# Keys and queries of the kept tokens: transposed by DMAs in place of VectorE

## The chip, the cores and the metric

The kernel runs on one core of a Trainium2 chip. That core has TensorE (matmuls; the profile calls it PE, its weight loads PEld), VectorE (DVE), ScalarE (ACT), GpSimd (POOL) and SyncE (SP), which issues DMAs. The five work side by side and wait for each other only by semaphores. The metric is the device time of one execution in microseconds; the time before is the median of 3 runs, 836.36 us (834.82 to 839.12).

## The reference

Two attention blocks read the same 2048 tokens of width 512, and a gate mixes them. Block A walks over 64 segments of 32 tokens, one after the other, because each hands 8 memory rows to the next:

```python
for s in range(n_seg):                       # 64
    xs = x[:, s*seg_len:(s+1)*seg_len, :]
    h = jnp.concatenate([mem, xs], axis=1)   # 8 memory rows + 32 tokens
    q = jnp.einsum('btd,dhe->bhte', h, Wq)   # 32 heads of 128; k and v alike
    scores = jnp.einsum('bhqe,bhke->bhqk', q, k) * scale
    scores = jnp.where(mask[None, None], scores, -1e9)
    o = jnp.einsum('bhqk,bhke->bhqe', _softmax(scores, axis=-1), v)
    o = jnp.einsum('bhte,hed->btd', o, Wo)
    mem = o[:, :M, :]
    outs.append(o[:, M:, :])
```

Block B is a causal attention with 32 heads of 16 within each of four stretches of 512 tokens, plus a running sum over the stretches before. The output is `g * a + (1 - g) * b`, with `g` a sigmoid of `x` times `gate_w`. All inputs are bf16.

## The kernel before

**Two kinds of tokens.** Of a segment's 40 rows (8 of memory, 32 tokens) the kernel takes 32 through the serial path: the 24 first tokens and the 8 memory rows, `hT`. The last 8 tokens of each segment do not depend on the memory until the scores, so their projections are made ahead, for four segments at a time: group `j` (0 to 15) holds the 4 x 8 last tokens of segments 4j to 4j+3. GpSimd gathers them into `xr` (`p_xr`), and `p_rest(j, kind, r)` projects them, for `kind` k, q or v and for `r`, the half of the heads (16 heads, 2048 columns).

**A projection.** `wproj` (L1389) makes it: the 32 tokens are the stationary side in four column tiles, so that partition 32g + t of the result holds token t and the g-th of four column sets of 512. For v a set is 512 neighbouring columns, four whole heads. For k and q a set is 32 of each head's 128 columns, for all 16 heads.

**The staging ring.** The result is copied out of PSUM (L995, by ScalarE or VectorE) into one of three staging buffers `stg`, taken in turn by `stage()`. The ring also serves block B's transposed keys (`bkn`, L1077), the second half of the output projection of the kept tokens (`parr`) and the rows of the final mix (`ain`, `fin`). For v a DMA stores the buffer to DRAM (`rvst`, L1361); it comes back spread over the segments as `rem_v` (`rlv`, L1398). For k and q VectorE transposes it in blocks of 32 x 32 (L1375) straight into `rem_k` or `rem_q`, 8 slots of [128, 256], one slot a segment, so that group j fills one half of the slots and group j+1 the other.

**A segment.** `p_seg(s)` copies the segment's kept queries out of `rem_q` into columns 32 to 39 of `QT` with one GpSimd copy (`qr`, L1422); the kept keys are read by TensorE where they lie in `rem_k` (L1464). Keys and queries of `hT` are projected, copied to `st` and transposed by VectorE (L1445). The scores `S` are the matmuls of L1460 and L1464. Then follow the exponentials (L1468), the sums `U` (L1483), their reciprocals on ScalarE (L1487, L1489), the multiplications (L1491 on VectorE, L1494 `nrr` on either VectorE or GpSimd), `PV` (L1525, L1530), the output projection (L1294), and `fold` and `hm` (L1018, L1317), which put the 8 new memory rows into the next `hT`.

**What sets the order.** Every operation is described once with its reads and writes. A planner can put them in order from costs written beside each (`cost`, and `load` for a DMA); here the order is given: `ORDER` is a packed table with one list for each engine, and each engine takes its list strictly in turn. An operation that either of two engines may do belongs to the one in whose list it stands. A slot of PSUM in pool "F" makes its first matmul wait for all that the later operations of the slot wait for, so a projection into a staging buffer that is not yet free holds TensorE's list. Operations on one named resource (`rem_k` of a parity, `stg1`, `qTr`) wait for each other.

```python
sl = P.slot("F" if j else "A")
P.op("dve", lambda d: d.transpose(dst, st[:, :].rearrange("p (h s k) -> p h s k", s=4, k=8)), reads=[rs],
     writes=["rem%s%d" % (kind, j % 2)], name="r%stp%d_%d" % (kind, j, r), cost=T_TP, prio=prio)
```

## Time and profile before

The profile shows one execution, which took 832.18 us, 830.2 us of them between its first and last instruction.

| what | us |
|---|---|
| median of 3 runs (lowest to highest) | 836.36 (834.82 to 839.12) |
| the profiled execution: time, span | 832.18, 830.2 |
| PE busy, share of the span | 805.0, 97% |
| PEld busy, share | 520.7, 63% |
| DVE busy, share | 623.3, 75% |
| ACT busy, share | 557.7, 67% |
| POOL busy, share | 256.8, 31% |
| the 64 transposes of kept keys and queries, VectorE (L1375) | 22.1 + 22.3 |
| the 64 copies of kept queries, GpSimd (L1422) | 27.4 |

A busy share is the union of an engine's instructions. Ends of matmuls are modelled and matmuls overlap, so a busy PE is not one at its peak. A row of waits reads "who waited <- for whom: us in total, times, longest us". A row of an instruction gives shortest, median and longest duration in ns, the first and last start in us, and its shape. "issue" is waiting that the profile can't put down to anyone. SyncE's entries are marked SPq: they issue DMAs and are not busy time.

### The profile page before, as it was taken

The numbers are of one execution on the slowest core, as the hardware profiler recorded it, in microseconds if no ns is written. First come the engines' busy times: TensorE is split into PE (matmuls) and PEld (weight loads), VectorE is DVE, ScalarE is ACT, GpSimd is POOL, SyncE is SP. The second block draws the span as 40 slices with busy tenths as digits, with TensorE's granted clock in tenths as the row PEclk, the third lists the DMA queues.
The fourth block names the chain that finished last, engine by engine and source line by source line (L and its number), as shares of the span: only waits on it lengthen the run. The fifth ranks groups of instructions, "written<-read, shape, count | busy, mean of one in ns | idle before, by whom it ended". The sixth has DMA issues, their size and how long they took to land.

```text
span 830.2 us, 53252 instructions
## 1 busy us (share of the span) xinstructions
PE 805.0 (97%) x24462; PEld 520.7 (63%) x24462; DVE 623.3 (75%) x1417; ACT 557.7 (67%) x1264; POOL 256.8 (31%) x572
## 2 busy tenths in 40 slices
PE   8999999999999999999999999999999999998988
PEld 4446666666566666666666666666666666665655
DVE  4878667778778778677787787777777867777776
ACT  3667666777667766667666767677677666666663
POOL 3453221333232323322322422423313314333240
PEclk9999999999999999999999999999999999999999
DMA  9983101111111110211012111101111100001001
GB/s 345 412 249 61 45 17 39 39 45 23 47 27 28 39 26 19 50 34 44 25 39 43 39 27 32 41 18 32 32 36 33 40 25 12 21 19 26 10 22 36
DMA packets 71700, 45.62 MB, mean 55 GB/s; under 512 B 50046, under 2 KB 69942, under 8 KB 69942
## 3 DMA queue, kind: packets, MB, share of 16 engines
q1 hardware_dynamic: 70422, 41.18, 17.2%
q8 instruction: 192, 3.15, 1.6%
q10 hardware_dynamic: 1056, 1.05, 0.4%
q14 instruction: 30, 0.25, 0.1%
HBM read 30.72 MB, written 8.87 MB: 48 GB/s over the span
## 4 chain that ended last, share of the span: by engine, by line
PE 82%; DMA 6%; DVE 4%; ACT 4%; SPq 2%; issue 1%; POOL 0%; DVEq 0%; POOLq 0%
PE pb L1389 45%; PE pb L1294 16%; PE pb L1018 7%; DMA Wo_sb<-in_A_Wo_dram 4%; PE pb L1135 3%; PE pb L1525 3%; PE pb L1020 2%; PE pb L1176 2%; PE pb L1483 2%; PE pb L1460 1%; SPq L891 1%; DMA rest_v<-stg 1%; DMA wqB_sb<-in_B_wq_dram 1%; PE pb L1224 1%; ACT rc_sb L1489 1%
## 5 line engine op out<-in xcount | busy, mean ns | idle before, releaser
L995 ACT ACTIVATE st<-pb 128x512 bf16<-128x512 f32 (+2 forms) x309 | 147.0, 495 | 115.8 <-PE pb L1389 96.4
L1153 ACT ACTIVATE PTB<-pb 128x640 bf16<-128x640 f32 x240 | 159.3, 703 | 46.3 <-PE pb L1135 37.3
L1389 PE MATMUL pb<-Wv_sb,hT 128*32 128x512 bf16 x2048 | 160.0, 379 | 0.0
L1389 PE MATMUL pb<-Wq_sb,hT 128*32 128x256 bf16 (+1 forms) x3072 | 139.0, 308 | 0.4 <-DVE hT L1317 0.4
L1389 PE MATMUL pb<-Wk_sb,hT 128*32 128x512 bf16 x2048 | 134.1, 379 | 0.7 <-DVE phiK L1204 0.7
L1294 PE MATMUL pb<-Wo_sb,OT_sb 128*32 128x256 bf16 x4096 | 130.7, 273 | 1.3 <-issue 0.8
L1294 PEld LDWEIGHTS pb<-Wo_sb,OT_sb 128*32 128x32 bf16 x4096 | 101.3, 96 | 14.3 <-ACT OT_sb L995 2.2
L1389 PEld LDWEIGHTS pb<-Wq_sb,hT 128*32 128x32 bf16 x3072 | 83.6, 97 | 41.1 <-issue 1.1
L1159 POOL TENSOR_SCALAR_AFFINE_SELECT PTB<-PTB 128x512 bf16<-128x512 bf16 x120 | 77.0, 642 | 95.6 <-ACT PTB L1153 89.2
L1445 DVE STREAM_TRANSPOSE QT_sb<-st 128x256 bf16<-128x256 bf16 (+1 forms) x192 | 94.1, 508 | 9.2 <-ACT st L995 7.4
L1445 DVE STREAM_TRANSPOSE KT_sb<-st 128x512 bf16<-128x512 bf16 x128 | 89.3, 700 | 12.4 <-ACT st L995 10.3
L1494 POOL TENSOR_TENSOR PT_sb<-PT_sb,rc_sb 128x64 bf16<-128x64 bf16 x87 | 32.0, 368 | 212.1 <-ACT rc_sb L1489 203.6
L1389 PEld LDWEIGHTS pb<-Wk_sb,hT 128*32 128x32 bf16 x2048 | 57.1, 97 | 44.0 <-issue 2.1
L995 ACT ACTIVATE OT_sb<-pb 128x320 bf16<-128x320 f32 (+1 forms) x141 | 57.8, 426 | 35.9 <-PE pb L1530 34.5
L995 DVE CAST OT_sb<-pb 128x320 bf16<-128x320 f32 (+1 forms) x119 | 56.5, 481 | 22.6 <-PE pb L1530 21.7
L1389 PEld LDWEIGHTS pb<-Wv_sb,hT 128*32 128x32 bf16 x2048 | 51.8, 96 | 18.5 <-ACT st L995 0.2
L1317 DVE CAST hT<-pb 128x32 bf16<-128x32 f32 x63 | 12.0, 190 | 68.3 <-PE pb L1018 68.1
L1487 ACT ACTIVATE rc_sb<-pb 128x160 f32<-128x160 f32 x128 | 38.9, 304 | 32.7 <-PE pb L1483 31.8
L1468 ACT ACTIVATE PT_sb<-pb 128x224 bf16<-128x224 f32 x128 | 45.4, 356 | 14.7 <-PE pb L1464 9.5
L1491 DVE TENSOR_TENSOR PT_sb<-PT_sb,rc_sb 128x160 bf16<-128x160 bf16 x128 | 43.0, 336 | 14.6 <-ACT rc_sb L1489 13.6
L995 DVE CAST V_sb<-pb 128x512 bf16<-128x512 f32 x60 | 40.9, 683 | 7.5 <-PE pb L1389 6.7
L1489 ACT ACTIVATE rc_sb<-rc_sb 128x160 f32<-128x160 f32 x128 | 43.0, 336 | 3.3
(199 smaller groups left out, 1464.6 us busy)
## 6 DMA issues: line engine op xcount, KB each, us to landing
Wv_sb<-in_A_Wv_dram SPq DMA_DIRECT2D x4, 1024.0 KB, 10.7
Wk_sb<-in_A_Wk_dram SPq DMA_DIRECT2D x4, 1024.0 KB, 19.2
Wq_sb<-in_A_Wq_dram SPq DMA_DIRECT2D x4, 1024.0 KB, 25.6
Wo_sb<-in_A_Wo_dram SPq DMA_DIRECT2D x4, 1024.0 KB, 22.5
rem_v<-rest_v SPq DMA_DIRECT2D x63, 64.0 KB, 2.9
rest_v<-stg SPq DMA_DIRECT2D x28, 128.0 KB
a_rows<-ao SPq DMA_DIRECT2D x63, 32.0 KB
stg<-a_rows SPq DMA_DIRECT2D x15, 128.0 KB
```

What stands on the lines that cost most here:

```text
L995: self.P.op(("act", "dve"), (lambda a: a.activation(dst, src(), ACT.Copy), lambda d: d.tensor_copy(dst, src())), reads=reads, writes=write ...
L1018: ins = pe.matmul(out[32 * c:32 * c + 32], lhsT[:, 32 * c:32 * c + 32], rhs, start=start, stop=stop, tile_position=(0, 32 * c), **kw)
L1153: P.op("act", (lambda dst=dst, src=src: lambda a: a.activation(dst, src(), ACT.Exp, scale=0.25))(), reads=[pair], writes=["%s%d_%d" % (nam ...
L1159: P.op("gp", (lambda pt=pt, ii=ii: (lambda g: g.affine_select(pt, pt, ([[0, len(ii)]] if len(ii) > 1 else []) + [[1, 128]], ALU.is_ge, 0.0 ...
L1294: ins = pe.matmul(pb[so.b][p0:p0 + 32, 0:256], tok(r, g, l), self.Wo[:, h, 256 * d:256 * d + 256], start=(r == 0 and g == 0 and l < 2), st ...
L1389: ins = pe.matmul(self.pb[sl.b][32 * g:32 * g + 32, 0:hi - lo], x[:, c, 0:32], cols, start=(c == 0), stop=(c == C - 1), tile_position=(0, ...
L1445: op("dve", (lambda dst=dst, src=src: lambda d: d.transpose(dst, src))(), reads=["st%d%s" % (i, tag)], writes=["%sT%d%s" % (kind, r, tag)] ...
L1468: op("act", lambda a: a.activation(PT[:, r, :], pb[rb.b][:, 0:224], ACT.Exp, scale=SCALE), reads=[rb], writes=["PT%d" % r, "PT%dr" % r], n ...
L1487: op("act", lambda a: a.activation(rc[:, r, :], pb[rb.b][:, 0:160], ACT.Ln), reads=[rb], writes=[rr], name="ln%d_%d" % (s, r), cost=t_act( ...
L1489: op("act", lambda a: a.activation(rc[:, r, :], rc[:, r, :], ACT.Exp, scale=-1.0), reads=[rr], writes=[rr], name="rc%d_%d" % (s, r), cost= ...
L1491: op("dve", lambda d: d.tensor_tensor(PT[:, r, 0:160], PT[:, r, 0:160], rc[:, r, :], ALU.mult), reads=[rp, rr], writes=[rp], name="nrm%d_% ...
L1494: op(("dve", "gp"), tuple((lambda e: e.tensor_tensor(rest, rest, late(rc[:, r, :]), ALU.mult)) for _ in range(2)), reads=[rp + "r", rr], w ...
```

## The change

For groups 4 to 15 (`j >= BYDVE`, 12 of 16) the buffer of k and q is no longer transposed by VectorE. A DMA transpose, issued by SyncE, moves it into the same tile `rem_k` or `rem_q`. For that the projection takes whole heads per column set (`heads=True`), as v does, and each 128 x 128 block of the buffer is one head in four. The result lies by head group and by token of all four segments, not by segment. So GpSimd copies it out for each segment from 16 on: the queries into `QT` (`qr`), now in two halves of 16 heads, and the keys into a new tile `Kc` (`kr`), also in two halves, which the score matmuls then read with the same shape as before. The resources are named by half. Some costs in the description are changed (`bkn`, `hx`, `qr`, `OTr`), and `ORDER` is a new table for all five engines. The matmuls are the same in number and shape.

```diff
     EARLY = 2
     BYPE = 4
+    BYDVE = 4
...
+        self.Kc = t("Kc", [128, 32, 8])
...
-                  writes=["stg%d" % b], name="bkn%d" % u, cost=0.5,
-                  load=1.5, prio=prio - 0.4)
+                  writes=["stg%d" % b], name="bkn%d" % u, cost=1.3,
+                  load=0.9, prio=prio - 0.4)
...
-        self.wproj(sl, kind, r, x, [rx], "r%s%d_%d" % (kind, j, r), prio, 4, j == 0)
+        self.wproj(sl, kind, r, x, [rx], "r%s%d_%d" % (kind, j, r), prio, 4, j == 0, heads=kind != "v" and j >= self.BYDVE)
...
+        if j >= self.BYDVE:
+            dst = self.rem[kind][:, 4 * (j % 2):4 * (j % 2) + 4, :].rearrange("p s x -> p (s x)")[:, 512 * r:512 * r + 512].rearrange("p (h x) -> p h x", h=4)
+            P.dma(group, lambda d: d.dma_start_transpose(dst, st[:, 0:512]), reads=[rs], writes=["rem%s%d_%d" % (kind, j % 2, r)], name="r%stp%d_%d" % (kind, j, r),
+                  cost=1.3, load=0.9, prio=prio)
+            return
...
-             writes=["rem%s%d" % (kind, j % 2)], name="r%stp%d_%d" % (kind, j, r), cost=T_TP, prio=prio)
+             writes=["rem%s%d_%d" % (kind, j % 2, r)], name="r%stp%d_%d" % (kind, j, r), cost=T_TP, prio=prio)
...
-                    part = part.rearrange("p (g x) -> p g x", g=4) if kind == "v" else part.rearrange("p (h g e) -> p g h e", g=4, e=32)
+                    part = part.rearrange("p (g x) -> p g x", g=4) if heads or kind == "v" else part.rearrange("p (h g e) -> p g h e", g=4, e=32)
...
+        if s >= 4 * self.BYDVE:
+            b0 = 4 * (s // 4 % 2)
+            Kr, Qr = (self.rem[k][:, b0:b0 + 4, :].rearrange("p s x -> p (s x)").rearrange("p (rh g t) -> p rh g t", g=4, t=32)[:, :, :, 8 * (s % 4):8 * (s % 4) + 8]
+                      for k in "kq")
+        rKr, rQr = (["rem%s%d_%d" % (k, s // 4 % 2, r) for r in range(2)] for k in "kq")
...
-        op("gp", lambda g: g.tensor_copy(QT[:, :, SEG:L], Qr.rearrange("p (h k) -> p h k", k=8)), reads=[rQr], writes=["qTr"],
-           name="qr%d" % s, cost=0.53, prio=s - 0.3)
+        if s >= 4 * self.BYDVE:
+            for r in range(2):
+                op("gp", lambda g, r=r: g.tensor_copy(QT[:, 16 * r:16 * r + 16, SEG:L].rearrange("p (g h) k -> p g h k", h=4),
+                                                      Qr[:, 4 * r:4 * r + 4].rearrange("p h g k -> p g h k")), reads=[rQr[r]], writes=["qTr%d" % r],
+                   name="qr%d_%d" % (s, r), cost=0.36, prio=s - 0.3)
+                op("gp", lambda g, r=r: g.tensor_copy(self.Kc[:, 16 * r:16 * r + 16, :].rearrange("p (g h) k -> p g h k", h=4),
+                                                      Kr[:, 4 * r:4 * r + 4].rearrange("p h g k -> p g h k")), reads=[rKr[r]], writes=["kc%d" % r],
+                   name="kr%d_%d" % (s, r), cost=0.36, prio=s - 0.3)
+            rKr = ["kc0", "kc1"]
+        else:
+            op("gp", lambda g: g.tensor_copy(QT[:, :, SEG:L], Qr), reads=rQr, writes=["qTr0", "qTr1"], name="qr%d" % s, cost=0.47, prio=s - 0.3)
+
+        def kr(r, g):
+            return (self.Kc if s >= 4 * self.BYDVE else Kr)[:, 16 * r + 4 * g:16 * r + 4 * g + 4, :].rearrange("p h k -> p (h k)")
...
-                    ins = pe.matmul(pb[rb.b][32 * g:32 * g + 32, 160:224], Kr[:, 8 * h0:8 * h0 + 32], QT[:, h0:h0 + 4, 24:40],
+                    ins = pe.matmul(pb[rb.b][32 * g:32 * g + 32, 160:224], kr(r, g), QT[:, h0:h0 + 4, 24:40],
```

More of the change, by code (lines that the diff above doesn't have):

```diff
@@ L1385, in f @@
                     part = w[:, c, 2048 * r:2048 * r + 2048]
-                    part = part.rearrange("p (g x) -> p g x", g=4) if kind == "v" else part.rearrange("p (h g e) -> p g h e", g=4, e=32)
+                    part = part.rearrange("p (g x) -> p g x", g=4) if heads or kind == "v" else part.rearrange("p (h g e) -> p g h e", g=4, e=32)
                     for g in range(4):
-                        cols = part[:, g] if kind == "v" else part[:, g, lo // 32:hi // 32]
+                        cols = part[:, g] if heads or kind == "v" else part[:, g, lo // 32:hi // 32]
                         ins = pe.matmul(self.pb[sl.b][32 * g:32 * g + 32, 0:hi - lo], x[:, c, 0:32], cols,
@@ L1411, in p_seg @@
         Vr, rVr = self.remv[par], "rem_v%d" % par
[L1412 to L1413 removed]
+        Kr, Qr = (self.rem[k][:, s % 8, :].rearrange("p (h k) -> p h k", k=8) for k in "kq")
+        if s >= 4 * self.BYDVE:
[3 more added lines that the diff above has]
+        rKr, rQr = (["rem%s%d_%d" % (k, s // 4 % 2, r) for r in range(2)] for k in "kq")
         sring = self.__dict__.setdefault("sring", [0])
```

144 lines of the change are left out of this document (72 added, 72 removed).

## The prediction

> **What bounds the kernel now.** I read the page first: span, busy time per engine, the queues. Then busy time by stretch, because the change only touches groups 4 to 15, whose work lies between about 205 and 760 us. Then the waits that ended last on the matmul stream and on the weight loads in that stretch, and last the rows of the operations that are taken out, moved or added.
>
> ```profile
> span 830.2 us, 53252 instructions
> PE 805.0 (97%) x24462; PEld 520.7 (63%) x24462; DVE 623.3 (75%) x1417; ACT 557.7 (67%) x1264; POOL 256.8 (31%) x572
> ...
> 205.00:760.00 555.00, 543.67 (x17036) 358.94 (x17032) 424.48 (x959) 380.84 (x866) 166.11 (x364) 1.00 0.13 32
> 760.00:830.20 70.20, 61.48 (x1985) 40.64 (x1977) 49.48 (x110) 41.84 (x105) 20.61 (x45) 1.00 0.08 22
> ```
>
> The columns of the last two rows are PE, PEld, DVE, ACT, POOL busy, the granted clock, DMA share and GB/s. In the stretch of the change TensorE is idle for 555.00 - 543.67 = 11.3 us. VectorE has 130 us to spare there, GpSimd 389, the DMA engines 87%. So nothing that the change removes is itself the bound; it can only shorten waits of TensorE. Those are:
>
> ```profile
> PEld pb L1525 <- issue: 15.9, 43, 0.6
> PEld pb L1483 <- ACT PT_sb L1468: 11.4, 44, 0.5
> PEld pb L1018 <- ACT st L995: 5.3, 14, 0.8
> PEld pb L1135 <- DVE PT_sb L1491: 4.8, 11, 0.6
> ...
> PEld pb L1389 <- DVE hT L1317: 2.5, 10, 0.4
> ...
> PEld pb L1460 <- DVE QT_sb L1445: 2.4, 10, 0.3
> PEld pb L1389 <- DMA rest_v<-stg: 2.3, 3, 0.8
> ```
>
> Adding all rows of this view that end on DVE (4.8 + 2.5 + 2.4 + 1.5 + 1.3 + 1.1 + 0.8) gives 14.4 us; on ACT 26.6 us. A weight load's wait is partly hidden by the matmul that still streams: the same view of the matmuls has only 1.8 us that end on DVE (0.7 + 0.5 + 0.4 + 0.2) and 3.7 on ACT. The last row shown is the staging ring: the next projection waited three times until a store out of `stg` had landed.
>
> **The change part by part.** The sum is made against the profiled execution: span 830.2, its time 832.18 us, 0.5% under the median 836.36 of the runs shown; I carry the difference over to the median unchanged.
>
> ```profile
> L1375 DVE STREAM_TRANSPOSE rem_k<-stg x32: 652/701/712, 33.8 to 754.5; 128x512 bf16<-128x512 bf16 x32
> L1077 SPq DMA_TRANSPOSE stg<-KT x8: 1190/1302/2097, 139.4 to 514.8; - x8
> DMA to landing us min/median/max: 2.6/3.4/4.8
> L1361 SPq DMA_DIRECT2D rest_v<-stg x28: 513/536/593, 73.7 to 723.8; - x28
> L1422 POOL COPY QT_sb<-rem_q x64: 396/397/677, 46.8 to 810.5; 128x256 bf16<-128x256 bf16 x64
> L1342 POOL COPY xr<-xT x16: 289/292/422, 10.1 to 634.8; 128x128 bf16<-128x128 bf16 x16
> ```
>
> (The landing row is that of the 12 transposes of x, which SyncE issues in 1.2 us like the 8 of KT8.)
>
> *Removed from VectorE.* 12 groups x 2 kinds x 2 halves = 48 transposes of 0.70 us: 33.6 us. The two order tables, decoded, also hand VectorE 7 more evictions of 512 columns (0.68 each; 11 more of V, 4 fewer of others), 6 more of 256 columns (0.43), 4 more of OT (0.48) and 3 more of the small products that GpSimd or VectorE may do (0.44): about 11 us. Net VectorE loses some 22.6 us, 5% of its 424 in the stretch. All of it lies beside TensorE. What it is worth is a share of the waits: at least 0, at most the 14.4 us of weight-load waits. I take a third, 5 us: the third of the way nearest to the 1.8 us of idle that the matmuls themselves show. What is late next where such a wait goes is ScalarE, whose waits are the larger ones.
>
> *Removed from ScalarE.* The same 17 evictions go (7 at 0.60, 6 at 0.38, 4 at 0.43): 8 us of 381, 2%. Of its 26.6 us of waits that is between 0 and 3; I take 1.5.
>
> *TensorE's work.* The same matmuls: 2914 entries in both tables. Projections of groups 4 to 15 read whole heads (contiguous columns) in place of 32-column strips 128 apart. The xr projections with strips (Wk, Wq) take 380 ns, those of V, contiguous, 380 ns: cost 0. The order is new: changes from one kind of operation to another rise from 1942 to 1960, changes of tile shape from 380 to 387. In the order of time, matmuls of one shape and different kind follow each other at 0.22 us a group of four, like within a kind; a change into the row tiles of L1525 starts 0.33 us after the group before, 0.11 more. So 25 changes cost between 0 and 25 x 0.11 = 2.8 us; I take 1.
>
> *Added to SyncE's queue.* 48 transposes x 1.30 = 62 us of issue (57 by the shortest row, 101 by the longest), where a v store took 0.54. SyncE only issues, so this is free unless something behind is wanted: the stores that free `stg` or `ao`, and the rem_v loads, which wait for PV two segments back and hold what stands behind them. In the new table rqtp7_0 and rqtp7_1 stand behind rlv29 while segment 28 needs them, with 20 entries of TensorE between rq7_0's last matmul and S28_0. An entry is 0.27 us (830.2 / 2914 is 0.28, with a slow start), so that is 5.4 us against eviction 0.6 + landing 3.4 + two copies 0.6. One wait of 0 to 2 us; I take 0.3. All other groups have at least 55 entries, 15 us. The DMA engines themselves, 13% busy, get 48 more transfers of 128 KB beside 154 stores and loads (28, 63 and 63 by the queue rows of the page): 0; the packets that load TensorE's instructions took 1.11 us near a transpose and 1.07 elsewhere in the trace, which at 48 of them is 2 us off the path, and up to 2 on it.
>
> *The staging ring.* A buffer used to be held for 0.6 + 0.7 us by a k or q; now 0.6 + 2.6 to 4.8, 4.0 at the median. The projection that uses it next waits on TensorE's own queue, since a slot of pool F takes over its later operations' conditions. Between the last matmul and that projection the old order leaves as little as 4 entries, the new one 17, 17, 17, 18, 18, 20, 22, 23, 24 and four times 25 (4.6 to 6.8 us), the other 15 more. A hold of 4.0 costs 0; of 5.4 (the longest landing) 3 x 0.8 + 2 x 0.5 = 3.4 us. Bounds 0 and 10.9 (below, first rival); I take 1, as most landings lie under 4.
>
> *Added to GpSimd.* 48 segments x 4 copies of 128 elements, 8 at a stride: the same pattern as the xr copy, 0.292, is 56.1 us; 48 copies of 0.397 go, 19.1 us: net +37, to 35% of the span. They wait for the scores of the segment before (the single Kc, QT), 8 us and more ahead of their use, but stand in one queue with the late multiplication (L1494, 87 times on GpSimd) that PV needs. Its engine waited 203.6 us for ScalarE, so the copies usually fit. Cost 0 to 48 x 0.28 = 13.4 (a copy of 0.677 beside one of 0.397, on the path each time); I take 0.5, near the bottom, since TensorE waited on GpSimd at L1525 for 1.9 us in all.
>
> Sum: -5 - 1.5 + 1 + 0.3 + 1 + 0.5 = -3.7 us, 828.5 for this execution, 832.7 as a median; I say 833.
>
> [...]
>
> **The rivals.**
>
> *Slower: the ring.* If a transpose is issued behind another (1.3 to 2.1 us) or lands late, the hold is 6.5 instead of 4.0, and the thirteen short handovers cost 3 x 1.9 + 2 x 1.6 + 1.1 + 0.6 + 0.3 = 10.9 us. It decides from a hold of about 5.5 us, 4.0 us in all. For it: 3 of the 28 v stores, through the same ring, stalled TensorE; two KT8 transposes took 2.0 us to issue. Against: the new order has spread these handovers. Net of the gains +2 to +12, some 843.
>
> *Faster by more.* TensorE's busy time hides waits. If all DVE waits of the weight loads shrink by two thirds and ACT's by a tenth, -9.6 - 2.7, plus 2.8 of costs: -9.5: 827; -15 if all of VectorE's go. For it: 14.4 against 1.8. Against: VectorE only loses 5%. [...]
>
> *Slower: GpSimd and VectorE block each other.* The 0.28 above in each of 48 segments, 13.4 us, less the gains: +1 to +13, some 845 at the full price. For it: copies of one size take 396 to 677 ns; against: their median is 397. [...]
>
> *No effect.* TensorE's list is as long as before, and the freed VectorE time was never waited for: -1 to +2, 836.5.
>
> **How the numbers follow.** Forecast (-9 to 0) 0.45, faster by more (-9 to -15) 0.16, ring 0.22, blocking 0.09, no effect 0.08. With 0.5% = 4.2 us, about what a measurement of this kernel can tell from no change: faster is 0.53 of the first and the second, 0.24 + 0.16 = 0.40; slower 0.78 of the ring and 0.7 of the blocking, 0.17 + 0.07 = 0.24; the rest, 0.36, within. The likeliest case's own range is 827 to 836.5. The range 824 to 844 leaves out four tenths of the larger gain (0.07) and four tenths of both slower ones (0.13).
>
> **What would show it.** Right: VectorE near 600 us, ScalarE near 550, GpSimd near 294; fewer rows of weight-load waits ended by DVE at L1135, L1389 and L1460; SyncE's transposes at 1.2 to 2.1 us; waits of L1389 on a DMA into `rem` under 4 us in all. Wrong towards slower: those DMA waits over 8 us, or L1525 waiting on GpSimd for far more than 1.9. Wrong altogether: TensorE's busy time itself differs by more than 5 us, which nothing here explains.

## The result and the profile after

The changed kernel takes 845.3 us at the median (843.27 to 850.11, 6 runs); the kernel before, timed beside it, takes 837.1 (834.82 to 839.12, 6 runs). The ratio is 1.0105, with a 95% interval of 1.0074 to 1.0135: one per cent slower, where I had forecast 833 and a gain. The execution profiled took 845.69 us, close to its median. The execution profiled of before, 832.18, lies 0.6% under its own, so 5 of the 13.8 us between the two spans are chance.

The page of the changed kernel, its span and busy times:

```profile
span 844.0 us, 53401 instructions
PE 811.5 (96%) x24441; PEld 521.9 (62%) x24441; DVE 609.3 (72%) x1389; ACT 551.8 (65%) x1247; POOL 292.1 (35%) x713
```

The loads of ScalarE and GpSimd came out as worked out, 552 us (I had 550) and 292 (294). VectorE came down to 609 us, by 14 and not by the 23 that I had worked out. TensorE's matmuls are 811.5 us busy instead of 805.0, though there are 21 fewer of them (24441 instead of 24462): some small operations are written for one tile or for four and take the shape of the entry before them, so "the same in number" holds for the 2914 entries of the list but not for the matmuls. The weight loads stay at 521.9 against 520.7.

Busy time in the stretch of the change, in the columns PE, PEld, DVE, ACT, POOL, clock, DMA share, GB/s, again of the changed kernel:

```profile
205.00:760.00 555.00, 537.98 (x16624) 351.10 (x16619) 396.37 (x903) 367.61 (x837) 195.06 (x481) 1.00 0.21 41
```

In the same 555 us TensorE now gets 16624 matmuls done instead of 17036: here the time is lost. The DMA engines are 21% busy instead of 13%. What the weight loads wait for in this stretch, and below two rows of the kernel before:

```profile
PEld pb L1550 <- issue: 13.4, 38, 0.7
PEld pb L1398 <- issue: 8.4, 14, 1.6
PEld pb L1139 <- DVE PT_sb L1516: 4.8, 15, 0.6
PEld pb L1298 <- issue: 4.4, 8, 1.0
...
PEld pb L1398 <- DMA rest_v<-stg: 3.3, 5, 1.0
...
PEld pb L1398 <- DVE hT L1321: 2.5, 8, 0.4
...
PEld pb L1485 <- DVE QT_sb L1470: 1.3, 4, 0.6
```

```profile
PEld pb L1389 <- issue: 1.9, 5, 0.7
...
PEld pb L1294 <- issue: 0.6, 1, 0.6
```

The lines are those of before moved by a few (L1389 is L1398, L1135 is L1139, L1460 is L1485, L1525 is L1550). Two things are to be seen. The three VectorE waits of the prediction were 4.8, 2.5 and 2.4; they are 4.8, 2.5 and 1.3. And the waits that the profile can put down to nobody have grown: at the projections from 1.9 to 8.4 us, at the output projection (L1294, now L1298) from 0.6 to 4.4, with single ones up to 1.6 us.

The operations that were added, SyncE's transposes by line and GpSimd's copies in the view of groups by form:

```profile
L1380 SPq DMA_TRANSPOSE rem_q<-stg x24: 1188/1229/2591, 188.1 to 767.6; - x24
L1380 SPq DMA_TRANSPOSE rem_k<-stg x24: 1191/1240/2717, 212.9 to 762.4; - x24
```

```profile
L1437 POOL COPY QT_sb<-rem_q 128x128 bf16<-128x128 bf16 x96 | 30.0, 312 | 28.5 <-PE pb L1489 17.1 <-PE pb L1022 3.7 <-DMA rem_q<-stg 1.4
L1440 POOL COPY Kc<-rem_k 128x128 bf16<-128x128 bf16 x96 | 29.4, 307 | 40.8 <-PE pb L1489 33.8 <-PE pb L1022 1.2 <-PE pb L1398 0.2
```

Each costs about what I had said (1.23 and 1.24 us of issue where I had 1.30, 0.31 us a copy where I had 0.29), and no projection waits for a transpose out of the staging ring: "DMA rest_v" is the store of v, as before. So neither addition takes longer than I had said, and still the kernel is slower.

**A wait that nobody is named for.** The longest stop in the changed kernel, first SyncE's timeline, then TensorE's weight loads and VectorE (start, duration, engine, line; in brackets the idle time before):

```profile
313.75 1.24 SPq L1380 DMA_TRANSPOSE rem_k<-stg  x1
315.03 1.27 SPq L1380 DMA_TRANSPOSE rem_q<-stg  x1
316.34 1.26 SPq L911 DMA_TRANSPOSE xT<-in_A_x_dram  x1
```

```profile
318.26 0.20 PEld L1022 LDWEIGHTS pb<-fold_sb,st 128*32 128x32 f32 x10 [0.34 <-ACT st L999]
...
320.19 0.15 PEld L1022 LDWEIGHTS pb<-fold_sb,st 128*32 128x32 f32 x6 [1.73 <-issue]
...
320.49 0.19 DVE L1321 CAST hT<-pb 128x32 bf16<-128x32 f32 x1 [2.66 <-PE pb L1022]
```

TensorE stops after 10 of 16 weight loads of one `fold`, for 1.73 us, with all of its inputs there. Counted from the start of the program, the next instruction has a number of the form 256 n + 193 or 194. Of the 21 stops over 0.5 us that the weight loads of this kernel have without a name after 60 us, 13 lie at such a number, where 2 in 256 would by chance. The page's table of queues has 192 packets on a queue of instructions, 3.15 MB, so 16 KB each; TensorE takes 49,000 instructions, so each packet is a block of 256. In the trace's packets the one that goes with this stop is moved from 316.98 to 318.84 us, 1.86 us in place of the 1.12 that they take on average, just after three transposes have been issued, and TensorE goes on 1.3 us after it has landed. This holds for every block: in nine profiles, of the kernel before, of the change and of runs below, TensorE passes some 184 such numbers each after 60 us, and never sooner than 1.19 us after the packet that goes with it has landed. So these stops are waits for instructions. Blocks are used up in some 4 us each (192 in 844 us); TensorE usually passes the number 2.0 to 2.2 us after the landing, so a packet that is a microsecond late is late for TensorE.

Adding up every wait of over 0.15 us at these places after 60 us, the kernel before has 7.4 us and, in a second profile, 7.9; the changed kernel has 16.3.

### The profile page after: what moved, and what is told of

It reads as the page before. It is cut to its first block, busy times and chain, and to the rows that moved or that the text cites. A ratio compares the mean times of both kernels' runs of the same rounds, so it can differ in the third digit from the quotient of the medians.

```text
span 844.0 us, 53401 instructions
## 1 busy us (share of the span) xinstructions
PE 811.5 (96%) x24441; PEld 521.9 (62%) x24441; DVE 609.3 (72%) x1389; ACT 551.8 (65%) x1247; POOL 292.1 (35%) x713
## 3 DMA queue, kind: packets, MB, share of 16 engines
q1 hardware_dynamic: 96534, 47.48, 23.3%
q8 instruction: 192, 3.15, 1.6%
## 4 chain that ended last, share of the span: by engine, by line
PE 83%; DMA 6%; DVE 3%; ACT 2%; issue 2%; SPq 2%; POOL 1%; DVEq 0%; POOLq 0%
PE pb L1398 44%; PE pb L1298 17%; PE pb L1022 7%; DMA Wo_sb<-in_A_Wo_dram 4%; PE pb L1139 3%; DMA rest_v<-stg 3%; PE pb L1550 3%; PE pb L1180 2%; PE pb L1024 2%; PE pb L1508 2%; SPq L895 2%; PE pb L1485 2%; PE pb L1228 1%; ACT st L999 1%; PE pb L1555 1%
## 5 line engine op out<-in xcount | busy, mean ns | idle before, releaser
L1398 PE MATMUL pb<-Wv_sb,hT 128*32 128x512 bf16 x2048 | 159.5, 379 | 1.3 <-issue 1.3
L1398 PE MATMUL pb<-Wq_sb,hT 128*32 128x512 bf16 (+1 forms) x3072 | 140.1, 308 | 0.5 <-DVE hT L1321 0.4
L1298 PE MATMUL pb<-Wo_sb,OT_sb 128*32 128x256 bf16 x4096 | 134.0, 273 | 2.5 <-issue 2.2
L1398 PE MATMUL pb<-Wk_sb,hT 128*32 128x512 bf16 x2048 | 133.7, 379 | 0.5 <-issue 0.5
L1298 PEld LDWEIGHTS pb<-Wo_sb,OT_sb 128*32 128x32 bf16 x4096 | 101.5, 96 | 18.1 <-issue 4.3
L1398 PEld LDWEIGHTS pb<-Wq_sb,hT 128*32 128x32 bf16 x3072 | 84.6, 97 | 40.8 <-DVE hT L1321 1.9
L999 DVE CAST OT_sb<-pb 128x320 bf16<-128x320 f32 (+1 forms) x123 | 58.7, 482 | 35.7 <-PE pb L1555 32.5
L1398 PEld LDWEIGHTS pb<-Wk_sb,hT 128*32 128x32 bf16 x2048 | 57.5, 97 | 41.1 <-issue 1.7
L1398 PEld LDWEIGHTS pb<-Wv_sb,hT 128*32 128x32 bf16 x2048 | 50.9, 96 | 20.6 <-issue 1.6
L999 DVE CAST V_sb<-pb 128x512 bf16<-128x512 f32 x71 | 48.5, 683 | 11.1 <-PE pb L1398 9.7
L1516 DVE TENSOR_TENSOR PT_sb<-PT_sb,rc_sb 128x160 bf16<-128x160 bf16 x128 | 44.3, 346 | 11.8 <-ACT rc_sb L1514 11.1
L1398 PE MATMUL pb<-Wq_sb,xr 128*32 128x512 bf16 x512 | 44.8, 380 | 1.9 <-DMA rest_v<-stg 1.1
```

The costliest lines, as they stand in the source:

```text
L999: self.P.op(("act", "dve"), (lambda a: a.activation(dst, src(), ACT.Copy), lambda d: d.tensor_copy(dst, src())), reads=reads, writes=write ...
L1298: ins = pe.matmul(pb[so.b][p0:p0 + 32, 0:256], tok(r, g, l), self.Wo[:, h, 256 * d:256 * d + 256], start=(r == 0 and g == 0 and l < 2), st ...
L1398: ins = pe.matmul(self.pb[sl.b][32 * g:32 * g + 32, 0:hi - lo], x[:, c, 0:32], cols, start=(c == 0), stop=(c == C - 1), tile_position=(0, ...
L1516: op("dve", lambda d: d.tensor_tensor(PT[:, r, 0:160], PT[:, r, 0:160], rc[:, r, :], ALU.mult), reads=[rp, rr], writes=[rp], name="nrm%d_% ...
```

## The experiments

Four theories stood. FETCH (the fetching of instructions): the transposes hold up the blocks of instructions. COPIES: GpSimd's 144 added copies delay what TensorE needs. QUEUE: SyncE's long issues, or the staging ring, delay stores and loads. ORDER: the new order costs, whatever it orders. All ratios are to the kernel before on the same chip.

**The change in the old order.** The changed kernel with before's lists; the transposes stand in SyncE's list behind the same neighbours as in the change.

```diff
-ORDER = (the table of the changed kernel)
+ORDER = (the table of before, each qr as qr_0, kr_0, qr_1, kr_1; the 48 transposes moved from VectorE's list to SyncE's)
```

> The change in the order of the kernel before: TensorE's, ScalarE's and VectorE's lists as they were (less the 48 transposes), the DMA transposes in SyncE's list where the changed kernel has them, four GpSimd copies where one stood. FETCH: about as slow as the changed kernel, 841 to 848. ORDER: back to 836 to 839. RING: slower than the changed kernel, over 848, since the old order leaves as little as 4 entries between a projection and the next user of its staging buffer; then TensorE's waits on a DMA at the rest projections exceed 8 us.

Measured: 880.81 us, ratio 1.0565 (1.054 to 1.059). TensorE's matmuls wait for:

```profile
PE pb L1397 <- DMA rem_k<-stg: 14.1, 7, 3.3
PE pb L1397 <- DMA rem_q<-stg: 13.1, 5, 5.1
```

This is the staging ring, my first rival, in its full size: twelve times a projection stands on TensorE's queue, up to 5 us, until a transpose has left the buffer. These waits are 27 of the 47 us. The granted clock was lower too: it was 0.986 in this profile, with 0.50 in six stretches of 3.4 or 6.8 us, 24 us in all, each beginning within 1.2 us of the end of such a wait. An estimate from these 24 us, if all that TensorE does there takes twice as long: up to 12 us. The change needs a new order, and the new order does take this away: in the changed kernel these rows are gone.

**DMA transposes added to before.** 96 transposes of [128, 256] into a tile of their own, in pairs where the change has its 48, that nobody reads.

```diff
+        for i, (anchor, nth) in enumerate(DUMMY):
+            o = P.dma(self.g_dum, lambda s: s.dma_start_transpose(self.dum[:, :, :], self.W["q"][:, 0, 0:256]), reads=["Wq0"], writes=["dum"], name="dum%d" % i, cost=0.7, load=0.5)
+            P.extras.append((o, anchor, nth))
```

> The kernel before, with its own order and its VectorE transposes, plus 96 DMA transposes of [128, 256] that nobody waits for (a constant piece of Wq into a spare tile), two behind each place in SyncE's list where the changed kernel has one: the DMA load of the change alone. Theory FETCH (DMA transposes delay the loads of TensorE's instructions, and TensorE runs dry at the end of a block of 256): slower by 5 to 9 us, 842 to 846, with more waits on 'issue' in the middle of a run of matmuls. Rival RING (the staging buffers are held longer): nothing reads or holds stg here, 836 to 838. Rival ORDER (the new order itself) and rival POOL (the added GpSimd copies): 836 to 838 as well.

Measured: 857.14 us, ratio 1.0274 (1.0243 to 1.0306), slower than any theory had it, and for another reason. The added operations and the matmuls' waits:

```profile
L783 SPq DMA_TRANSPOSE dum<-Wq_sb x96: 1168/1180/2413, 187.7 to 788.9; - x96
```

```profile
PE pb L1407 <- DMA rest_v<-stg: 8.1, 7, 2.1
PE pb L1036 <- DVE st L1013: 5.9, 1, 5.9
```

A transpose of half the size costs SyncE as much, 1.18 us, so this kernel has 113 us of added issue in place of 60, and the stores behind it come late: QUEUE, at twice its dose. Here too the granted clock was halved, for 10 us (0.994 over the profile), around waits of 5.9 and 2.1 us, which by the same estimate is worth up to 5 of the 24 us. The waits at instruction blocks came to 8.8 us, hardly more than before's. The kernel was a bad test of FETCH, since it changed two doses at once. A store of v costs the projections 3.3 us of waits in the change against 2.3 before, so at the change's own dose QUEUE is worth about a microsecond.

**The change with small transfers.** Each transpose is a plain DMA of 16 columns; order and copies stay.

```diff
-            P.dma(group, lambda d: d.dma_start_transpose(dst, st[:, 0:512]), ...
+            P.dma(group, lambda d: d.dma_start(dst[:, 0, 0:16], st[:, 0:16]), ...
```

> The changed kernel in its own order, but each of the 48 DMA transposes is a plain DMA of 16 columns (4 KB) into the same tile; the rest of the transposed keys and queries is not written, which leaves that part of the computation out. FETCH: most of the loss goes, 835 to 840. RING: it also goes, if the shorter landing is what counts; then the waits on a DMA at the rest projections vanish. ORDER and POOL: stays at 843 to 847.

Measured: 840.94 us, ratio 1.008 (1.0048 to 1.0112). At the middle of the interval three quarters of the loss stay without any of the transposes, so FETCH and QUEUE are unlikely to be the main cause.

**The new order with VectorE's transposes.** First with the split copies, then with before's one copy and the keys read in place, which is before's work in the new order.

```diff
-        ... heads=kind != "v" and j >= self.BYDVE)
+        ... heads=False)      # strips, as before
-        if j >= self.BYDVE:
+        if False:             # VectorE transposes again, placed in its list by the time of the DMA
...
-    BYDVE = 4                 # the second kernel also: one copy, keys in place
+    BYDVE = 99
```

> The changed kernel in its new order, with the split GpSimd copies of queries and keys, but the 48 transposes back on VectorE (inserted where the DMA stood in time), the layout of the tile as before. FETCH: 834 to 839, no DMA load is left. RING: the same. ORDER and POOL: 843 to 847, since the order of the four other engines and the 144 more GpSimd copies are kept.

> The operations of the kernel before (VectorE transposes, one copy of the queries, the keys read in place) in the changed kernel's order; only the resources are named by half, so that the order is possible. Theory ORDER: slower than before by 5 us or more, ratio 1.006 to 1.014. Theory COPIES and theory QUEUE: within 2 us of before, apart from waits on VectorE's transposes, which this order does not plan for and which the trace shows by name.

Measured: 845.99 us, ratio 1.0143 (1.0118 to 1.0168), and 847.1, ratio 1.0131 (1.0097 to 1.0165). Against the change's 1.0096 (all its runs together, see the table below) the first is slower by 0.47% (0.30 either way), the second by 0.35% (0.38), which may be noise. In the first:

```profile
PE pb L1483 <- DVE KT_sb L1468: 3.3, 8, 0.9
```

Adding up the matmuls' waits over 0.15 us after 60 us, those on VectorE are 8.8 us (22 times) and 8.3 us (21), against 3.4 us (9) in the second profile of the change: the new order leaves no room for these transposes. The waits without a name are 3.2 and 5.5 us against 9.3 (the stops at instruction blocks are 8.0 and 10.8 us here, 13.7 there). So in this order taking the work off VectorE does pay: the first, with the same copies, is slower by 0.61% (0.32 either way) than the change with small transfers and real copies (1.0082 below), where VectorE is relieved. But the same work is faster still in before's own order. The second kernel has none of the additions and is 11 us slower than before. Part of this is VectorE, on which its matmuls wait 8.3 us (3.1 in before) and its weight loads 35.2 (22.7).

**Copies alone.** Before's order and transposes, with the change's copies.

```diff
-        op("gp", lambda g: g.tensor_copy(QT[:, :, SEG:L], ...), name="qr%d" % s)
+        for r in range(2):      # from segment 16 on
+            op("gp", ... QT[:, 16 * r:16 * r + 16, SEG:L] ..., name="qr%d_%d" % (s, r))
+            op("gp", ... self.Kc[:, 16 * r:16 * r + 16, :] ..., name="kr%d_%d" % (s, r))
```

> The kernel before, in its own order and with VectorE's transposes, but with the changed kernel's GpSimd work: from segment 16 on the kept queries are copied in two halves and the kept keys are copied into Kc, 144 more copies, each at the place where the one copy stood. Theory COPIES (the added copies are what costs; GpSimd's queue gets longer, and VectorE is slowed by it): 4 to 9 us slower than before, ratio 1.005 to 1.011, with waits of TensorE on GpSimd (scores on Kc, PV on the late multiplication) up by several us. Theory ORDER (the new sequence of all engines costs, whatever the operations are): within 2 us of before, ratio 0.998 to 1.003. Theory QUEUE (SyncE's 1.2 us a transpose and their landing cost): also within 2 us.

Measured: 844.19 us, ratio 1.009 (1.0059 to 1.0122): as much as the whole change, as COPIES had it. The matmuls' waits in this kernel and, below, in the kernel before:

```profile
PE pb L1021 <- issue: 4.3, 6, 1.1
PE pb L1547 <- POOL PT_sb L1516: 3.6, 6, 1.0
```

```profile
PE pb L1018 <- issue: 2.2, 4, 0.6
...
PE pb L1525 <- POOL PT_sb L1494: 1.1, 2, 0.9
```

PV waits longer for the multiplication that stands behind the copies in GpSimd's queue. Over the matmuls' waits above 0.15 us after 60 us, those on GpSimd rise from 1.1 to 5.4 us, those on VectorE from 3.1 to 3.6, and those that nobody is named for from 3.2 to 8.3 (the stops at instruction blocks of the weight loads are 14.3 us here), part of it chance (see below): this profile lies 3 us above the kernel's median, and that of before under its own. VectorE's own busy time grew by only 1.1 us (624.4 against 623.3), and its multiplications (L1491) take 336 ns in both, so the copies don't make its instructions longer.

**VectorE relieved, nothing else.** The 48 transposes of before move 32 columns in place of 512.

```diff
+        n = 16 if j < 4 else 1
-        P.op("dve", lambda d: d.transpose(dst, st[:, :].rearrange("p (h s k) -> p h s k", s=4, k=8)), reads=[rs],
+        P.op("dve", lambda d: d.transpose(dst[:, 0:n], st[:, 0:32 * n].rearrange("p (h s k) -> p h s k", s=4, k=8)), reads=[rs],
```

> The kernel before, in its own order; the 48 VectorE transposes of groups 4 to 15 move 32 columns in place of 512, so the rest of the kept keys and queries is left as it was (that part of the computation is left out). This measures by itself what freeing VectorE is worth, the first term of my sum: 5 us faster (0 to 14.4), ratio 0.994. If VectorE's waits are not on the path, the ratio is 0.998 to 1.000, and the waits of the weight loads that end on VectorE shrink by less than 3 us.

Measured: 835.86 us against 835.89, ratio 0.9998 (0.9977 to 1.0019). Its page:

```profile
PE 806.7 (96%) x24462; PEld 524.3 (63%) x24462; DVE 602.9 (72%) x1417; ACT 558.2 (67%) x1264; POOL 256.2 (31%) x572
```

Twenty microseconds off VectorE change the time by nothing that can be seen: -1.9 to +1.6 us. The three waits of the prediction that end on VectorE (L1389 and L1460 are L1390 and L1461 here), in the stretch:

```profile
PEld pb L1135 <- DVE PT_sb L1492: 4.8, 11, 0.6
...
PEld pb L1390 <- DVE hT L1317: 2.3, 9, 0.4
PEld pb L1461 <- DVE QT_sb L1446: 2.3, 10, 0.3
```

They are 4.8, 2.3 and 2.3 us where before has 4.8, 2.5 and 2.4. So they end on VectorE without VectorE being late through other work. This holds for before's order, which was made with these transposes in it; in the new order, as seen above, they do cost.

**Chance in the profile.** The two kernels profiled once more.

> The changed kernel once more, as the measure for the three runs beside it. Expected 1.008 to 1.013 times the kernel before, some 842 to 847 us.

> The kernel before once more, for a second profile: the stops of TensorE at block boundaries of its instructions came to 7.4 us in the first one and to 12.1 and 14.3 us in two kernels with the same TensorE list. If this sum only scatters from run to run, it is expected anywhere from 7 to 14 us; if it belongs to the kernel, near 7.4.

Measured: ratios 1.0092 (1.006 to 1.0124) and 1.0006 (0.9989 to 1.0023). The stops at instruction blocks were 13.7 us in the changed kernel (16.3 at first) and 7.9 in before (7.4). They were 12.1 in the kernel with small VectorE transposes, which is as fast as before: a single profile of this sum is good to some 3 us, and single stops of 1.1 us come and go.

**The new order with small additions, and the square around it.** In the changed kernel's order: both additions small, only the transposes real, only the copies real (the run above), and the change.

```diff
+                nk = 4 if s == 16 else 1      # copies small: 8 elements from segment 17 on
-... QT[:, 16 * r:16 * r + 16, SEG:L].rearrange("p (g h) k -> p g h k", h=4)
+... QT[:, 16 * r:16 * r + 4 * nk, SEG:L].rearrange("p (g h) k -> p g h k", h=4)[:, :, 0:nk]
...
-            P.dma(group, lambda d: d.dma_start_transpose(dst, st[:, 0:512]), ...      # transposes small
+            P.dma(group, lambda d: d.dma_start(dst[:, 0, 0:16], st[:, 0:16]), ...
```

> The changed kernel in its own order, with both additions made small: each of SyncE's 48 transposes is a plain transfer of 16 columns, and the 192 GpSimd copies of keys and queries from segment 17 on move 8 elements (most of the kept keys and queries are left out of the computation). What is left is the new order with VectorE freed. Theory ORDER: still 1.006 or more. Theory ADDITIONS (copies and transposes, by queueing and by the loading of instructions, make up the whole loss): 0.998 to 1.003, some 836 us.

> The changed kernel in its own order with its real DMA transposes, but the 192 GpSimd copies small, as in the run beside it (which leaves most of the kept keys and queries out of the computation). Its difference to that run is the price of the transposes: theory FETCH 4 to 6 us, as the places where both profiles of the changed kernel were behind all others in this order add up to 6.4 us; theory COPIES under 2 us. Its difference to the changed kernel is the price of the copies: COPIES 4 to 8 us, FETCH under 2.

> First of four runs of one square, all in the changed kernel's order and on one chip: transposes small or real, copies small or real. This one has both small (most of the kept keys and queries are left out of the computation). Expected 1.004 times the kernel before, as measured once.

> Real DMA transposes, small copies (most of the kept keys and queries left out). If the two additions cost each by itself and add up: 1.007 to 1.009 here, with the difference to both small equal to the difference between the changed kernel and the run with real copies alone. If each only uses up the same slack: as much above both small as the changed kernel itself.

> Small transfers in place of the transposes (kept keys and queries left out), real copies. Adding up: 1.006 to 1.008, and the changed kernel is above it by what the transposes cost alone. Same slack: 1.008 to 1.010, the changed kernel no more than 0.1% above.

> The changed kernel: 1.009 to 1.011. Adding up: above both small by the sum of the two differences. Its profile should again show TensorE stopping near 318, 440, 444 and 581 us at block boundaries of its instructions, where only kernels with the real transposes stopped.

The ratios, with the stops at instruction blocks (us, added up from the trace) of each profile:

| in the new order | ratios | weighted | stops |
|---|---|---|---|
| both small | 1.0042 (1.0026 to 1.0058), 1.0068 (1.0044 to 1.0092) | 1.0050 | 8.0, 8.8 |
| transposes real | 1.0092 (1.007 to 1.0114), 1.0099 (1.0073 to 1.0124) | 1.0095 | 9.6, 11.8 |
| copies real | 1.008 (1.0048 to 1.0112), 1.0083 (1.0058 to 1.0109) | 1.0082 | 9.9, 10.2 |
| both real: the change | 1.0105 (1.0074 to 1.0135), 1.0092 (1.006 to 1.0124), 1.0092 (1.0068 to 1.0116) | 1.0096 | 16.3, 13.7, 11.9 |

The weights are the inverse squares of the intervals; the weighted ratios are good to 0.13, 0.17, 0.20 and 0.16%. The order with both additions small costs 0.5%, 4.2 of 8.0 us, although VectorE and ScalarE are relieved in it. It is not the order alone: a copy of 8 elements still takes 0.19 us where a real one takes 0.31, and a small transfer 0.53 us of issue where a transpose takes 1.23. GpSimd's copies are 47 us in all in this kernel, 66 in the change and 27 in before, so half of the added copy time is still there. GpSimd's busy time lies between before's 256.8 and the change's 292.1 us:

```profile
PE 808.0 (97%) x24441; PEld 520.6 (62%) x24441; DVE 607.6 (73%) x1389; ACT 550.7 (66%) x1247; POOL 271.5 (33%) x713
```

An estimate, if what is left of the additions costs in proportion to its time: 19 us of added copy time are left and 20 are taken away, for the 0.32% below; 0.53 us of issue are left of each transfer and 0.70 are taken away, for 0.45%. What is left would then be worth about 0.3% each, as much as the 0.5%. So the square gives the order no price of its own, and no run has the new order with VectorE relieved and no additions at all. The transposes add 0.45% (0.21 either way), the copies 0.32% (0.24), both together 0.46%: less than the sum of 0.77%, which points to one slack that either uses up, but the gap of 0.31% is just within its interval (0.33%), so this is not settled.

In this order the block at 318 us shows FETCH at one place. With small transfers and small copies the weight loads' stop there is 0.4 us; with the real transposes it is 1.7 to 2.0 us in each of five profiles; without them 0.4 to 1.0 us in each of six. The kernel with both small, TensorE's timeline:

```profile
317.03 0.27 PE L1022 MATMUL pb<-fold_sb,st 128*32 128x16 f32 x9
317.63 0.25 PE L1022 MATMUL pb<-fold_sb,st 128*32 128x16 f32 x7 [0.33 <-issue]
```

The packet of that block took 0.93 us here and 1.84 with the transposes (1.86 in the change). But the third profile of the change has the same stop with a packet of 1.14 us. It set out late, 0.5 us before the fold's first load, where the other four with transposes set out 1.2 to 1.4 before it and both small 1.8:

```profile
317.35 0.20 PEld L1022 LDWEIGHTS pb<-fold_sb,st 128*32 128x32 f32 x10 [0.34 <-ACT st L999]
319.33 0.15 PEld L1022 LDWEIGHTS pb<-fold_sb,st 128*32 128x32 f32 x6 [1.78 <-issue]
```

What the five have in common is the landing: 0.6 or 0.7 us after the fold's first load, where the six without the transposes have it 0.3 to 0.9 us before. TensorE goes on 1.3 to 1.7 us after the landing in all eleven. Another block, at 440 us, stops by 0.8 us in four of the five profiles with transposes and in none without. So at these blocks transposes do delay instructions. In the sum it shows less clearly, since copies raise it too: 8.4 us at the mean with both small, 10.7 with the transposes, 10.1 with the copies, 14.0 in the change, and a single profile scatters by 3. Not all of a stop of a weight load is idle time of the matmuls: in the first profile of the change the stop of 1.73 us leaves them idle for 1.66, one of 1.09 at 391 us for 0.80. A long stop may also cost more than itself: after the longest of the five, 2.04 us with real transposes and small copies, the granted clock was 0.50 for 3.4 us, with 48 matmuls in them where the first profile of the change has 88 in the same 3.4 us at 1.00 (columns as above, the clock third from the end):

```profile
321.00:324.40 3.40, 3.40 (x48) 1.76 (x44) 2.56 (x6) 1.80 (x4) 1.84 (x5) 0.50 0.05 14
```

The other profiles of the square have no such stretch; their granted clock is 1.000.

**Why the order would cost: changes of shape?** What grew from before (second profile) to both small were, again, waits without a name, at changes into another kind of matmul:

```profile
PEld pb L1135 <- issue: 5.5, 18, 0.5
...
PEld pb L1460 <- issue: 1.0, 4, 0.4
```

```profile
PEld pb L1139 <- issue: 8.0, 28, 0.5
...
PEld pb L1486 <- issue: 4.8, 21, 0.4
```

Over all weight loads after 60 us these waits rose from 35.8 to 41.9 and 42.3 us (both profiles with both small) with the stops at blocks unchanged, and those on VectorE from 23.3 to 28.4 and 27.3, with VectorE less busy; those on ScalarE fell from 40.0 to 37. They go with the order: away from block numbers the weight loads' nameless waits are 28 us in before, 34 with both small and 36 in the kernel with before's work in the new order, which has no addition; at the two lines shown it has 6.5 and 4.8 us, both small 6.0 and 4.5, before 2.7 and 1.0. How much of a weight load's wait reaches the end is not known. In the trace of before a PV after a projection starts loading 0.52 us after it, a PV after block B's scores (row tiles too) 0.10. So I tested the price of a change of shape in before's own list of TensorE: 35 places with two changes more, 29 places where a score block of block B moves as far with none, and 32 places with two changes fewer. One place of each:

```diff
-wo25_0, bL8_2, PV25_1
+bL8_2, wo25_0, PV25_1
...
-fold26, bL8_1, rv8_0_3
+bL8_1, fold26, rv8_0_3
...
-PV26_1, wo26_0, ..., fold26, bL8_1
+PV26_1, bL8_1, wo26_0, ..., fold26
```

> The kernel before with 35 places of TensorE's list altered: where one operation X is followed by a score block of block B (L1135, row tiles) and this by PV (L1525, row tiles), X and the score block change places. Nothing else moves, PV stays where it is; but X now stands between two operations on row tiles, so there is one change out of them and one into them more at each place, 70 in all. By my price of a change (0 to 0.11 us) that is 0 to 7.7 us. By the spacing of weight loads in the trace of before (projection to PV 0.52 us against 0.10 from block B's scores to PV, and 0.24 from block B's scores to a projection against 0.10 between others) it is about 0.5 us a place, some 18 us: ratio 1.015 to 1.025.

> The control of the run beside it: at 29 places where a score block of block B stands alone between other operations, it changes places with the one before it. The number of changes stays the same and the lists move as much. By both prices within 3 us of before, ratio 0.997 to 1.004; if it is as slow as the run beside it, moving a score block is what costs, and not the change of shape.

> The kernel before with fewer changes: 32 score blocks of block B that stand alone up to 14 entries behind a PV are put straight behind that PV, ahead of the output projection. That takes away one change into row tiles and one out of them at each place. By the spacings in the trace (0.14 to 0.52 us in, 0.24 out, against 0.10 without) it should gain 0.2 to 0.4 us a place, 6 to 13 us, less what the output projection starts later (0.1 to 0.2 us a place, 3 to 6 us): ratio 0.988 to 1.000. By my price it is between 7 us faster and 6 us slower. It would be a version that beats both kernels.

Measured: 839.93 us, ratio 1.0078 (1.0053 to 1.0104); 837.72, ratio 1.0068 (1.0039 to 1.0096); 926.68, ratio 1.1121 (1.1078 to 1.1163). The price by the spacing of weight loads falls: 70 more changes cost 6.5 us (4.4 to 8.7), 0.12 each at the most, even if nothing is put down to the moving, and the control, with none more, is as slow within the intervals. What the control pays for is another thing. Of its weight loads, and those of before below:

```profile
PEld pb L1389 <- DVE hT L1317: 7.2, 23, 0.4
...
PEld pb L1135 <- ACT st L995: 3.2, 8, 0.4
```

```profile
PEld pb L1389 <- DVE hT L1317: 2.8, 12, 0.4
```

Moving 29 score blocks forward by a single entry, a quarter of a microsecond, makes other work come too early or too late; which of the moves cost most was not separated. The third kernel shows how far this goes: its score blocks stand up to 14 entries ahead of where ScalarE's list expects them, and TensorE waits for the exponentials that must first empty a bank:

```profile
PE pb L1136 <- ACT PTB L1154: 42.5, 23, 2.2
PE pb L1295 <- ACT PTB L1154: 10.9, 8, 1.9
```

These two rows are 53 of the 93 us. The granted clock was 0.957 in this profile: it was halved for 79 us in all, mostly for 3.4 us at a time and, in most cases, beginning within 2 us after a stop of 1 to 2 us, which by the same estimate is worth up to 40 us.

No version that beats both kernels came out of this. Relieving VectorE gains nothing in before's order; whether an order between the two would gain was not tried.

## Why the prediction was wrong

- **VectorE's relief, -5 us (0 to 14.4): the step that failed first.** Relief alone, in before's order, is worth 0.0 (-1.9 to +1.6). I read "ended on VectorE" as "would end earlier if VectorE had less to do" and took a third of those waits. The low end of my bounds was right. The profile of before had the sign of it: VectorE had 130 us to spare in the stretch, and the matmuls' own waits on it were 1.8 us. Two smaller slips did not matter beside this: the 14.4 us are the sum of the longest rows of the view (all rows that end on VectorE make 17.3), and VectorE's busy time fell by 14 us instead of 23.
- **TensorE's work, +1 us (0 to 2.8): the second.** I priced the new order by its 25 more changes of kind and shape. The price of a change (I had up to 0.11 us, at most 0.12 was measured) was right; the idea that an order is worth the sum of its changes was not. The new order costs 4.2 us with the reliefs in it and both additions small, where my sum had -5.5 for the three terms together. Some ten of the twelve microseconds between forecast and result are these two steps, with what is left of the additions. How much of the 4.2 us is the order and how much is left of the additions is not shown. That the order has a part in it is likely, since the weight loads wait longer at changes of kind in it even without any addition; by what exactly, beyond the rows above (waits at changes of kind and on VectorE's results), stays open. The 29 moves show only that before's lists fit the durations so closely that a quarter of a microsecond at 29 places costs 0.7%.
- **Instruction packets, 0 ("2 us off the path, and up to 2 on it"): undersized.** I took the mean, 1.11 against 1.07 us. What counts is the single packet that lands late, because it takes longer or because it sets out later: at one block the stop is 1.7 to 2.0 us with the transposes and 0.4 with both additions small. The stops rise by 5.6 us between both small and the change, from both additions; the transposes by themselves cost 3.8 us (0.45%, 0.21 either way) above both small, of which the stops are a part.
- **GpSimd, +0.5 us (0 to 13.4): undersized.** The copies fit their queue by time, but not where the multiplication stands behind them. In the old order they cost 7.5 us (0.9%), in the new one at least 2.7 (0.32%, 0.24 either way, against copies that are small but not gone). In the new order the matmuls' waits on GpSimd are 1.0 us, as before (1.1), so there the way by which the copies cost is not shown. The 0.677 us beside 0.397 that the range was built on was not the way it went.
- **SyncE and the staging ring, +0.3 and +1 us: right.** One copy of queries waits for a DMA, 1.4 us, once, as worked out for segment 28 within 0 to 2; no projection waits for a transpose. The rival "ring" has nearly the right time (843) and the wrong mechanism, which is luck. It is real in the old order, where the change costs 47 us.
- **ScalarE, -1.5 us (0 to 3):** waits on it did fall by some 3 us in the weight loads; what of it reached the end can't be told apart from the order.
- **The rival "GpSimd and VectorE block each other"** gave 845, the measured time, by luck: its mechanism did not show. With the copies in the old order VectorE's multiplications take as long as before; in the change they take 346 ns instead of 336, 1.3 us in all.
- **"Wrong altogether: TensorE's busy time differs by more than 5 us"** was a bad sign to choose. With the same matmuls it is 804.9 in the kernel before, 809.9 with the copies and 811.0 with 35 moves, while the weight loads stay between 518 and 522. So busy matmul time contains waits here, 5 to 6 us more of them in these two kernels.

## What to carry to other kernels

A wait that ends on an engine is not a wait that goes when this engine gets less to do: shrink the work in place and time it before moving it elsewhere. When a change comes with a new order, time the new order by itself, with everything added made small, and look at how much of the additions is still there; here that kernel had half of the loss and half of the added copy time, and 29 moves by one entry in a list that fits closely cost 0.7%, not much less than the change. A wait that nobody is named for, in the middle of a run of equal instructions, is worth counting against the number of the instruction: at 256 n plus a constant it was the loading of instructions here, and at one block the stop was 1.7 to 2.0 us in each of five profiles with real transposes, 0.4 to 1.0 us in each of six without.

## What the runs showed of the hardware

In both kernels TensorE's 49,000 instructions came in 192 packets of 16 KB, 256 at a time, of 1.07 us on average in the kernel before and 1.12 in the changed one. Of the 21 nameless stops over 0.5 us in the first profile of the changed kernel, 13 stand at one place of a block, its number 193 or 194 of 256. TensorE went on 1.19 us or more after the landing, every time in nine profiles. These stops add up to about 8 us in the kernel before and 12 to 16 in the changed one, with single stops of 0.2 to 2 us.

The granted clock was halved at long stops of TensorE in four profiles, mostly for 3.4 or 6.8 us at a time: for 10, 24 and 79 us in all in those of the three slowest kernels (0.994, 0.986 and 0.957 over the profile), and once for 3.4 us after a stop of 2.04 us for instructions (0.998). In the profiles of before (two) and of the change (three) it is 1.000, after a stop of 1.73 us too.

The DMA queue's rows show what the transposes bring, first of the kernel before, then of the changed one (packets, MB, share of 16 engines):

```profile
q1 hardware_dynamic: 70422, 41.18, 17.2%
q8 instruction: 192, 3.15, 1.6%
```

```profile
q1 hardware_dynamic: 96534, 47.48, 23.3%
q8 instruction: 192, 3.15, 1.6%
```

48 transposes of 128 KB bring 26,112 packets, 544 each, and 6.3 MB: over a third more packets for a seventh more bytes. And a DMA transpose costs SyncE the same for [128, 256] as for [128, 512], 1.18 against 1.23 us at the median, where a plain transfer of 16 columns costs 0.53; so 96 of half the size took 113 us of issue where the 48 take 60.
